# Cluster products, one-hot turns and weight conversions take other tiles of a hand-written attention schedule

## The chip, the cores and the metric

The kernel runs on one core of one Trainium2 chip. The metric is the device time of one execution in microseconds (us); the number that counts is the median of several runs. The core has five engines that run their own instruction queues in order: TensorE (PE in the views, its weight loads PEld), VectorE (DVE), ScalarE (ACT), GpSimd (POOL) and SyncE (SP), which here issues the DMAs.

## The reference

Clustered attention, then two feed-forward stages, all in float32:

```python
q_assign = np.argmax(np.einsum('bhsd,hcd->bhsc', q_n, c_n), axis=-1)   # nearest of 16 centroids
k_assign = np.argmax(np.einsum('bhsd,hcd->bhsc', k_n, c_n), axis=-1)
mask = q_assign[:, :, :, None] == k_assign[:, :, None, :]
scores = np.where(mask, scale * np.matmul(q, k.transpose(0, 1, 3, 2)), -1000000000.0)
attn = softmax(scores)                                  # over keys
x = np.matmul(attn, v)                                  # q, k, v: 2 batches, 8 heads, 768, 64
x = relu(x @ w_in) ** 2 @ w_out                         # 1536 tokens, 512 -> 2048 -> 512
out = sum(p[:, e:e+1] * (relu(x @ w1[e]) @ w2[e]) for e in range(4))
```

## The kernel before

**Stages.** Attention comes first (to about 300 us of the span), then the two feed-forward stages as one long run of matmuls. Every float32 operand is split into a rounded high part and a low part, and products are made of both.

**Attention by tiles.** 16 heads (2 batches by 8) of 6 tiles of 128 queries are 96 tiles, counted by `g`. In tile `g` the program issues: the score products of tile `g+2` (emit_S, L574), the row maximum of tile `g+2` on VectorE (L583), the exponential of tile `g+1` on ScalarE (L594), the turn (transposition) of tile `g`'s probabilities in two halves of three 128x128 transposes (L607), whose results ScalarE (L612, high part `pth`) and VectorE (L613, low part `ptl`) take out of PSUM, and half of the products with `v` of an earlier pair of tiles (L621, L623). The order of these inside a tile is written out by hand in `ORDER`, one list for even and one for odd tiles: `S`, `M`, `E`, `T0`, `T1`, `H`/`L` (results of the turns), `P` (products with `v`), `O` (their results), `R` (loads and DMAs from the table `early`), `C` (one step of the assignment chain from the list `dq`), `K` (one step of a weight conversion). `X1` and `X2` are two places for work of the next heads; `Y1` and `Y2` take their results out of PSUM. All the work at X1 and X2 goes through one PSUM tile, `m`, of a pool with one buffer.

**The preparation of a pair of heads.** Two heads are prepared together, and their work is spread over the 12 tiles before. The tables `AT` (relative to the pair's first tile) and `START` (for the first such pair) say in which tile. I count these 12 tiles as positions 0 to 11, so position 0 is 12 tiles ahead, position 10 two tiles ahead. The parts are:

- turns of k and q (trans_slot, L354), two each at positions 10 and 11 of the cycle before: ScalarE copies each result into `kqf` (L361, three buffers), and GpSimd makes the high and low parts from it (round_pool at L52, then L363) as `nkh`, `nkl`, `nqh`, `nql`;
- cluster products in two halves (pair_scores, L404): keys and queries against the centroids, four matmuls each; ScalarE copies the result to `ys` (L410);
- turns of `ys` in two halves (pair_turn, L420), summed on VectorE into `A` (L425). The second one puts the assignment chain on `dq`: maximum (L456) on VectorE, three GpSimd operations (L446 to L448), two empty steps, second maximum (L457) on VectorE, four GpSimd operations (L451 to L454) that write the one-hot rows `oh`;
- the one-hot turn (pair_hot, L480): `oh` is transposed, ScalarE copies it to `ohm` (L485), and four DMAs (hot_rows, L497) lay its rows under the stacked operands `q2` and `k2` of the pair's first head. The second matmul pair of emit_S reads these;
- stacking DMAs (stack, L375 and L377) that copy parts of `nkh`, `nkl`, `nqh`, `nql` into operands.

The normaliser of the pair that has just ended (norm_slots) uses the same places: its four small VectorE steps (L663 to L666) are put at the head of `dq` at position 2, its turn (L672) comes at position 5, its two broadcasts (L689) at positions 8 and 9. The end of an odd tile issues a DMA of results (L649, `xm`) at position 7.

**The weight conversions.** The first feed-forward weights arrive as 64-bit words, which five VectorE operations (L160, L163, L166, L171, L176, on 128x512 elements), a ScalarE copy and a GpSimd subtraction turn into float32 parts (split64). 24 such steps (four blocks of six) lie in the list `cq` and are done one at a time at `K`, from tile 8 on (`AT["conv"]`). When `cq` is empty, `K` issues pieces of the next weights (`lq`) in tiles with `g % 6 == 4`.

Of the kernel before, what the change touches and what calls it, by code (L numbers as in the profile page):

```python
# [22 lines left out]

ORDER = [
    "S T0 X1 M E T1 R Y1 X2 H0 P0 C H1 L0 L1 C K Y2".split(),
    "S X1 E M T0 T1 Y1 H0 C P1 X2 R L0 H1 C L1 O Y2 C".split()]
WARM = [12, 10, 5, 11, 3, 9]
START = {'t': [0, 1, 1, 2], 'a': [3, 4, 4, 5, 7], 'stack1': 4, 'stack': 5, 'head': [0, 2]}
AT = {"gap": 2, "stack1": -11, "stack": -9, "ohd": -7, "splitv": -3, "load": -8,
      "t": [-14, -14, -13, -13], "a": [-12, -11, -11, -10, -5], "conv": 8}  # L30


@with_exitstack
def moe_attention_kernel(
# [19 lines left out]
    B, H, S, D = q.shape  # L54
    C = centroids.shape[1]
    NT, DM = out.shape
    E = moe2_w1.shape[0]
# [66 lines left out]
    def w_loads(ci):  # L124
        return [(ci, part, half) for part in range(2) for half in range(2)]
# [73 lines left out]
    with tc.manual_schedule():  # L199
# [87 lines left out]
        dq = []  # L287
# [91 lines left out]
        def assign_slot(i):  # L379
            def f():  # L380
                m = ps_m.tile([128, 2 * NTT, 2 * C], F32, tag="m", name="m")
                for j, nm in enumerate(("k1", "q0")):
                    for t in range(NTT):
                        nc.tensor.matmul(
                            m[:, j * NTT + t], stk[i, nm][:, t * 128:(t + 1) * 128],
                            cc[:, i % H], start=True, stop=True)

                def evac():
                    A = as_p.tile([128, 4 * NTT, C], F32, tag="A", name="A")[:, 0:2 * NTT]
                    nc.vector.reduce_sum(  # L390
                        out=A, in_=m.rearrange("p t (s c) -> p t c s", s=2), axis=AX.X)
                    dq.extend(onehot_ops(i, A))
                return evac
            return f
# [130 lines left out]
        def onehot_slot(i):  # L525

            def f():
                while dq:
                    dq.pop(0)()
                om = as_p.tile([128, HALF], F32R, tag="ohm", name="ohm")[0:4 * C]  # L530
                m = ps_m.tile([4 * C, HALF], F32R, tag="m", name="m")
                for a in range(QT):
                    nc.tensor.transpose(
                        m[:, a * 128:(a + 1) * 128],
                        ohs[i][:, 2 * a:2 * a + 2].rearrange("p t s c -> p (t s c)"), identr)

                def evac():
                    nc.scalar.copy(om, m.bitcast(F32))
                    for s, nm in enumerate(("q2", "k2")):
                        for e in range(2):  # L540
                            r = (2 * e + s) * C
                            nc.sync.dma_start(
                                out=stk[i, nm][D:D + C].bitcast(F32).rearrange(
                                    "c (a e n) -> c a e n", a=QT, e=2)[:, :, e],
                                in_=om[r:r + C].bitcast(F32).rearrange("c (a n) -> c a n", a=QT))
                return evac
            return f
# [490 lines left out]
        early, slots = {}, {}  # L1038

        def at(d, g, f):  # L1040
            d.setdefault(max(g, 0), []).append(f)

        for i in range(1, NH):
            u0 = i * NTT
            if i > 1:
                for n, x in enumerate(("stack1", "stack")):
                    at(early, START[x] if i == 2 else u0 + AT[x], lambda i=i, n=n: stack(i, n))
                if i % 2:
                    at(early, u0 + AT["ohd"], lambda i=i: hot_rows(i))
            else:  # L1050
                for n in range(2):
                    at(slots, START["head"][n], onehot_slot(i) if n else assign_slot(i))
            at(early, u0 + AT["splitv"], lambda i=i: split_v(i))
            if i + 1 < NH:
                at(early, u0 + AT["splitv"] + 1, lambda i=i: load_v(i + 1))
        for j in range(1, NH // 2):
            u0 = 2 * j * NTT
            for n, f in enumerate(pair_slots(j)):
                at(slots, START["t"][n] if j == 1 else u0 + AT["t"][n], f)
            for n, f in enumerate([pair_scores(j, 0), pair_scores(j, 1), pair_turn(j, 0),  # L1060
                                   pair_turn(j, 1), pair_hot(j)]):
                at(slots, START["a"][n] if j == 1 else u0 + AT["a"][n], f)
            if j + 1 < NH // 2:
                at(early, u0 + AT["load"], lambda j=j: load_pair(j + 1))
        at(early, 4, lambda: load_w(*w_loads(0)[1]))
        cq, lq = [], []
        for j in range(NF):
# [5 lines left out]
        for g in range(NU):  # L1073
            par = g % 2
            todo = slots.pop(g, [])
            if nq:
                f = nq.pop(0)
                if f is not None:
                    todo.append(f)
            pr, w = divmod(g - 2, 2)  # L1080
            has_pv = 0 <= pr < NU // 2
            end = {}

            def slot(n):
                if todo:
                    end[n] = todo.pop(0)()

            def T(half):
                if g < NU:
                    end["H%d" % half], end["L%d" % half] = emit_T(g, half)  # L1090

            def PV(half):
                if has_pv and w == half:
                    emit_PV(pr, half)

            def PO():
                if has_pv and w == 1:
                    emit_PO(pr)
                    ii, jj = divmod(pr, NTT // 2)
                    if ii % 2 == 1 and jj == NTT // 2 - 1 and pr + 1 < NU // 2:  # L1100
                        nq.extend(norm_slots(ii // 2))

            def other():
                for f in early.pop(g, []):
                    f()

            def convert():
                if g >= AT["conv"] and cq:
                    cq.pop(0)()
                elif not cq and g % NTT == 4:  # L1110
                    for _ in range(2):
                        lq and lq.pop(0)()

            def finish(n):
                f = end.pop(n, None)
                if f:
                    f()

            do = {
                "E": lambda: emit_exp(g + 1), "S": lambda: emit_S(g + 2),  # L1120
                "M": lambda: emit_max(g + 2), "P0": lambda: PV(0), "P1": lambda: PV(1),
                "O": PO, "R": other, "T0": lambda: T(0), "T1": lambda: T(1),
                "X1": lambda: slot("Y1"), "X2": lambda: slot("Y2"),
                "C": lambda: dq and dq.pop(0)(),
                "K": convert,
            }
            for a in ORDER[par]:
                do[a]() if a in do else finish(a)
            while todo:
                whole(todo.pop(0))  # L1130
            if g == NU - 2:
                prep.close()
                mctx = ExitStack()
                for nm in ("w01", "g", "tp"):
                    mp[nm] = mctx.enter_context(
                        tc.tile_pool(name=nm, bufs=1, reuse_waits="tile"))
                w_pool[0, 1] = mp["w01"]
                ga = mp["g"].tile([128, 12 * TB], F32R, name="ga")
                mp["g1"] = ga.rearrange("p (k x t) -> p k x t", k=6, x=2)
                mp["g2"] = ga.rearrange("p (k t) -> p k t", t=HALF)  # L1140
                fa = mp["tp"].tile([128, 6 * HALF + 1024], F32, name="fa")
                mp["r"] = fa[:, 0:2 * TB].rearrange("p (k t) -> p k t", k=2)
                mp["c"] = fa[:, 0:6 * HALF].rearrange("p (k t) -> p k t", k=6)
                sa = fa[:, 6 * HALF:6 * HALF + 1024]
                mp["s"] = sa.rearrange("p (s k f) -> p s k f", s=4, k=2)
                cv_p.append(lambda shp: sa[:, 0:512] if len(shp) == 2 else
                            sa[:, 0:512].rearrange("p (k f) -> p k f", k=shp[1]))
# [55 lines left out]
        def r_ops(b, ops):  # L1203
# [8 lines left out]
        head = {  # L1212
            -1: [("t", RT3), ("t", RT1), ("h", RT1), ("t", RT2), ("l", RT1)],
            0: [("h", RT2), ("h", RT3), ("t", RT4), ("l", RT2)],
            1: [("l", RT3), ("h", RT4), ("h", RB22)],
            2: [("l", RT4), ("l", RB22)]}
# [89 lines left out]
```

## Time and profile before

| | |
|---|---|
| median of 3 runs | 1063.62 us (1061.05 to 1064.61) |
| the profiled execution | 1067.48 us, its span 1065.7 us |
| TensorE busy in the span | 1035.0 us, 97% |
| VectorE, ScalarE, GpSimd busy | 64%, 51%, 52% |
| granted TensorE clock, mean | 0.991 of full |

Busy time of TensorE counts matmuls whose ends are modelled, so 97% doesn't mean that it runs at its peak: a matmul that waits for its predecessor's results shows as a gap, one at a lower clock shows as busy. The span is split at about 300 us: ahead of that all four engines work on attention, after it TensorE has no gap.

### The profile page before, as it was taken

To read this page: it belongs to the slowest core of one execution; us is meant where nothing else is said; L and a number is where in the kernel's file an instruction comes from. 1 tells how busy PE (TensorE), PEld (TensorE's weight loads), DVE (VectorE), ACT (ScalarE), POOL (GpSimd) and SP (SyncE) were. 2 spreads that over 40 slices of the span, in tenths; PEclk is the share of its full clock that TensorE was granted. 3 is DMA by queue.
4 is the path that set the end of the run, shared out by engine and by line. 5 is a ranking of instruction groups with operands and counts; after the bars stand their busy time and mean duration, and the time that the engine had idled before them with its cause. 6 is when DMAs were issued, how large, how long until landed. Compare 5 with 4: busy or idle time off the path is not lost.

```text
span 1065.7 us, 14971 instructions
## 1 busy us (share of the span) xinstructions
PE 1035.0 (97%) x5558; PEld 913.1 (86%) x5558; DVE 684.6 (64%) x1074; ACT 539.7 (51%) x1080; POOL 558.5 (52%) x543
## 2 busy tenths in 40 slices
PE   8899898899999999999999999999999999999998
PEld 7788787888978888888888888899988888889987
DVE  7787787687967676472145555567767555555654
ACT  6678787788855554444344343333354334333331
POOL 3256755665322222224447666667767666666650
PEclk9899999999999999999999999999999999999999
DMA  4664645475212322120102112212213221221201
GB/s 116 146 144 107 139 105 131 112 188 122 48 40 79 113 86 79 40 84 36 40 1 80 65 55 79 79 40 80 79 48 132 79 68 51 79 80 40 79 1 60
DMA packets 72409, 86.07 MB, mean 81 GB/s; under 512 B 26896, under 2 KB 49744, under 8 KB 72336
## 3 DMA queue, kind: packets, MB, share of 16 engines
q1 hardware_dynamic: 72336, 85.11, 28.0%
q8 instruction: 44, 0.72, 0.3%
q14 instruction: 29, 0.24, 0.1%
HBM read 59.83 MB, written 3.15 MB: 59 GB/s over the span
## 4 chain that ended last, share of the span: by engine, by line
PE 83%; DVE 9%; POOL 4%; DMA 2%; issue 1%; ACT 1%; SPq 0%; POOLq 0%; DVEq 0%; ACTq 0%
PE bank L897 25%; PE bank L857 21%; PE bank L750 12%; PE bank L732 4%; PE bank L733 4%; PE bank L731 4%; PE s L574 3%; PE t L607 3%; DVE ptl L613 3%; DVE nb L583 2%; PE po L621 2%; PE po L623 2%; DMA k<-nkh 1%; PE m L404 1%; PE m L689 1%
## 5 line engine op out<-in xcount | busy, mean ns | idle before, releaser
L897 PE MATMUL bank<-w1h,ga 128*128 128x512 f32 x768 | 269.9, 393 | 0.0
L907 DVE SCALAR_TENSOR_TENSOR x<-bank,pe_p,x 128x512 f32<-128x512 f32 x180 | 134.8, 750 | 167.5 <-PE bank L897 167.5
L857 PE MATMUL bank<-xa,w0h 128*128 128x384 f32 x896 | 228.3, 335 | 0.1
L857 PEld LDWEIGHTS bank<-xa,w0h 128*128 128x128 f32 x896 | 164.5, 188 | 17.9 <-ACT fa L868 0.5
L897 PEld LDWEIGHTS bank<-w1h,ga 128*128 128x128 f32 x768 | 144.1, 188 | 24.5
L740 POOL TENSOR_TENSOR ga<-fa,ga 128x512 fp32r<-128x512 f32 x48 | 62.5, 1302 | 177.6 <-ACT ga L739 135.1
L897 PE MATMUL bank<-w1l,ga 128*128 128x512 f32 x384 | 151.6, 395 | 0.0
L857 PE MATMUL bank<-xa,w0l 128*128 128x384 f32 x448 | 149.7, 334 | 0.0
L868 ACT COPY fa<-bank 128x384 f32<-128x384 f32 x96 | 45.6, 475 | 171.6 <-PE bank L857 171.6
L613 DVE TENSOR_TENSOR ptl<-t,pth 128x384 fp32r<-128x384 f32 x192 | 98.8, 549 | 43.8 <-ACT pth L612 43.4
L750 PE MATMUL bank<-ga,w1h 128*128 128x512 f32 x384 | 126.5, 389 | 0.0
L877 ACT ACTIVATE ga<-fa 128x384 fp32r<-128x384 f32 x96 | 50.5, 526 | 135.5 <-DVE fa L871 135.5
L826 POOL TENSOR_TENSOR w0l<-raw,w0h 128x512 fp32r<-128x512 f32 x64 | 75.0, 1194 | 81.2 <-ACT w0h L825 81.2
L844 POOL TENSOR_TENSOR w1l<-raw,w1h 128x1024 fp32r<-128x1024 f32 x32 | 77.3, 2414 | 71.3 <-ACT w1h L843 71.3
L583 DVE TENSOR_REDUCE nb<-s 128x1 f32<-128x768 f32 x96 | 91.2, 950 | 14.9 <-PE s L574 14.2
L607 PE MATMUL t<-identf,p 128*128 128x128 f32 x576 | 89.5, 280 | 6.4 <-DVE ptl L613 5.8
L612 ACT CAST pth<-t 128x384 fp32r<-128x384 f32 x192 | 85.0, 486 | 12.0 <-PE t L607 10.5
L594 ACT ACTIVATE p<-s,nb 128x768 f32<-128x768 f32 x96 | 87.3, 910 | 6.2 <-DVE nb L583 6.0
L880 DVE SCALAR_TENSOR_TENSOR ga<-fa,ga 128x384 fp32r<-128x384 f32 x96 | 90.1, 938 | 0.6 <-ACT ga L877 0.6
L574 PE MATMUL s<-k,q 80*128 80x384 f32 (+1 forms) x384 | 87.7, 351 | 0.2 <-DVE q L327 0.2
L737 ACT ACTIVATE fa<-bank 128x512 f32<-128x512 f32 x44 | 26.4, 599 | 118.0 <-PE bank L733 116.6
L750 PEld LDWEIGHTS bank<-ga,w1h 128*128 128x128 f32 x384 | 72.1, 188 | 14.8
(204 smaller groups left out, 2081.4 us busy)
## 6 DMA issues: line engine op xcount, KB each, us to landing
raw<-in_moe_w_dram SPq DMA_DIRECT2D x64, 512.0 KB, 4.0
raw<-in_moe_w_in_dram SPq DMA_DIRECT2D x8, 1024.0 KB, 5.3
raw<-in_moe_w_out_dram SPq DMA_DIRECT2D x6, 1024.0 KB, 5.0
k<-nkh SPq DMA_DIRECT2D x28, 192.0 KB, 3.3
q<-nqh SPq DMA_DIRECT2D x28, 192.0 KB, 3.6
nv<-in_v_dram SPq DMA_DIRECT2D x16, 192.0 KB, 3.8
out_dram<-x SPq DMA_DIRECT2D x12, 256.0 KB, 2.2
k<-nkl SPq DMA_DIRECT2D x14, 192.0 KB, 3.0
```

The lines of the kernel that those rows point to most:

```text
L574: nc.tensor.matmul(s[:, j, 0:HALF], stk[i, nq][:, t * 128:(t + 1) * 128], stk[i, nk][:, j * HALF:(j + 1) * HALF], start=first, stop=not first)
L583: nc.vector.tensor_reduce(out=nb, in_=s_ps[u][:, :, 0:HALF], axis=AX.XY, op=ALU.max, negate=True)
L594: nc.scalar.activation(p, s_ps.pop(u)[:, :, 0:HALF], AF.Exp, bias=nb_t.pop(u), accum_out=sums_t[hp][:, i % 2, t:t + 1])
L607: nc.tensor.transpose(tp[:, j], p_sb[u][:, half, j * 128:(j + 1) * 128], identf)
L612: return (lambda: nc.scalar.copy(dh, tp), lambda: nc.vector.tensor_tensor(dl, tp, dh.bitcast(F32), op=ALU.subtract))
L613: lambda: nc.vector.tensor_tensor(dl, tp, dh.bitcast(F32), op=ALU.subtract))
L750: nc.tensor.matmul(o, a, b, start=(ft == 0 and z == 0), stop=(ft == NF - 1 and z == 2))
L844: nc.gpsimd.tensor_tensor(lo, w, hi.bitcast(F32), op=ALU.subtract)
L857: nc.tensor.matmul(ps, w[:, o:o + 128], r_op(r, x)[:, kt], start=(first and kt == 0 and z == 0), stop=(kt == 1 and z == 2), skip_group_che ...
L880: nc.vector.scalar_tensor_tensor(out=g_t(n, f, t, 1), in0=h_src(n, f, t), scalar=0.0, in1=g_t(n, f, t, 0).bitcast(F32), op0=ALU.max, op1=A ...
L897: nc.tensor.matmul(o, a, w[:, f], start=(f == 0 and z == 0), stop=(f == 1 and z == 2))
L907: nc.vector.scalar_tensor_tensor(out=acc, in0=o, scalar=pc, in1=acc, op0=ALU.mult, op1=ALU.add)
```

## The change

Four things change. In `AT` and `START` the two cluster products move from positions 0 and 1 to position 2 (both), the turns from positions 1 and 2 to positions 3 and 4, the one-hot turn from position 7 to position 8. For the first such pair the second product and second turn come one tile earlier, and the one-hot turn of head 1 (onehot_slot) takes the second place of its tile. `K` stands in odd tiles too. And `K` does a conversion step only while `dq` is empty.

```diff
-    "S X1 E M T0 T1 Y1 H0 C P1 X2 R L0 H1 C L1 O Y2 C".split()]
+    "S X1 E M T0 T1 Y1 H0 C P1 X2 R L0 H1 C L1 O K Y2 C".split()]
-START = {'t': [0, 1, 1, 2], 'a': [3, 4, 4, 5, 7], 'stack1': 4, 'stack': 5, 'head': [0, 2]}
+START = {'t': [0, 1, 1, 2], 'a': [3, 3, 4, 4, 7], 'stack1': 4, 'stack': 5, 'head': [0, 2]}
-      "t": [-14, -14, -13, -13], "a": [-12, -11, -11, -10, -5], "conv": 8}
+      "t": [-14, -14, -13, -13], "a": [-10, -10, -9, -8, -4], "conv": 8}
...
-                for n in range(2):
-                    at(slots, START["head"][n], onehot_slot(i) if n else assign_slot(i))
+                at(slots, START["head"][0], assign_slot(i))
...
+        at(slots, START["head"][1], onehot_slot(1))
...
                 if g >= AT["conv"] and cq:
-                    cq.pop(0)()
+                    if not dq:
+                        cq.pop(0)()
```

On TensorE, position 0 of the second such pair (tile 12) stood like this before; the four L404 rows are the first half of the cluster products, and the L621 and L623 rows that follow are the products with `v`:

```order
L574 MATMUL s<-k_600,q_663 128x384 x2
L574 MATMUL s<-k_666,q_668 128x384 x2
L607 MATMUL t<-identf,p 128x128 x3
L404 MATMUL m<-nkh,cp 128x384
L404 MATMUL m<-nkl,cp 128x384
L404 MATMUL m<-nqh,cp 128x384
L404 MATMUL m<-nql,cp 128x384
L607 MATMUL t<-identf,p 128x128 x3
```

Of the change, TensorE at position 2 (tile 14):

```order
L574 MATMUL s<-k_605,q_663 128x384 x2
L574 MATMUL s<-k_666,q_668 128x384 x2
L607 MATMUL t<-identf,p 128x128 x3
L404 MATMUL m<-nkh,cp 128x384
L404 MATMUL m<-nkl,cp 128x384
L404 MATMUL m<-nqh,cp 128x384
L404 MATMUL m<-nql,cp 128x384
L607 MATMUL t<-identf,p 128x128 x3
L404 MATMUL m<-nkh,cp 128x384
L404 MATMUL m<-nkl,cp 128x384
L404 MATMUL m<-nqh,cp 128x384
L404 MATMUL m<-nql,cp 128x384
```

The same eight rows now stand two tiles later, and the second half follows in the same tile after only three transposes.

On VectorE, positions 4 to 7 of that pair before; L456 and L457 are the chain's two maxima, L176 is a conversion step:

```order
L456 TENSOR_REDUCE mx<-A 128x24
L583 TENSOR_REDUCE nb<-s 128x1
L613 TENSOR_TENSOR ptl<-t,pth 128x3x128 x2
L176 SCALAR_TENSOR_TENSOR cva<-raw,cva 128x512
L583 TENSOR_REDUCE nb<-s 128x1
L613 TENSOR_TENSOR ptl<-t,pth 128x3x128
L457 TENSOR_REDUCE mx_1557<-A 128x24
L613 TENSOR_TENSOR ptl<-t,pth 128x3x128
L583 TENSOR_REDUCE nb<-s 128x1
```

Of the change, VectorE from the same maximum on (positions 4 to 7); L163 and L166 are conversion steps:

```order
L456 TENSOR_REDUCE mx<-A 128x24
L583 TENSOR_REDUCE nb<-s 128x1
L613 TENSOR_TENSOR ptl<-t,pth 128x3x128 x2
L583 TENSOR_REDUCE nb<-s 128x1
L457 TENSOR_REDUCE mx_1127<-A 128x24
L613 TENSOR_TENSOR ptl<-t,pth 128x3x128 x2
L163 TENSOR_SCALAR cva<-cva 128x512
L583 TENSOR_REDUCE nb<-s 128x1
L613 TENSOR_TENSOR ptl<-t,pth 128x3x128 x2
L166 TENSOR_SCALAR cva<-cva 128x512
```

The conversion between the two maxima is gone, and one conversion stands in each tile from the second maximum's on.

On SyncE's queue, the DMAs around the one-hot rows (`ohm`) of that pair before:

```order
L497 DMA q_1089<-ohm 16x3x128 x2
L497 DMA k_1087<-ohm 16x3x128 x2
L375 DMA k_1247<-nkh 64x768
L377 DMA k_1247<-nkl 64x768
L649 DMA xm<-xs 64x768
L375 DMA q_1335<-nqh 64x768
```

And of the change:

```order
L375 DMA k_1240<-nkh 64x768
L377 DMA k_1240<-nkl 64x768
L649 DMA xm<-xs 64x768
L497 DMA q_1085<-ohm 16x3x128 x2
L497 DMA k_1083<-ohm 16x3x128 x2
L375 DMA q_1338<-nqh 64x768
```

The four one-hot DMAs have moved behind three others, two of the next head's stack and the one of results.

## Rows read from the trace of the kernel before

**Rows 1.** Windows of ten tiles, positions 0 to 9, of six pairs; columns as printed.

```profile
core 0: us, PE busy (x) PEld busy (x) DVE busy (x) ACT busy (x) POOL busy (x), PEclk, DMA share, GB/s
59.66:87.68 28.02, 26.00 (x188) 23.29 (x186) 23.62 (x43) 22.83 (x53) 16.51 (x22) 1.00 0.50 113
93.60:122.02 28.42, 25.98 (x187) 23.30 (x186) 23.61 (x43) 22.84 (x53) 16.92 (x23) 1.00 0.49 109
127.94:158.44 30.50, 27.72 (x188) 24.88 (x186) 23.71 (x43) 22.86 (x53) 17.42 (x23) 0.94 0.44 98
164.36:195.38 31.02, 27.77 (x188) 24.78 (x186) 23.25 (x42) 22.84 (x53) 17.90 (x24) 0.94 0.47 109
201.30:231.51 30.21, 27.27 (x187) 24.89 (x186) 20.95 (x39) 22.01 (x52) 16.46 (x25) 0.94 0.56 136
237.43:264.64 27.21, 25.50 (x187) 23.38 (x186) 20.86 (x39) 21.92 (x52) 15.06 (x24) 1.00 0.49 121
```

**Rows 2.** Windows of single tiles: positions 0 and 1, position 1, a plain tile.

```profile
201.30:207.59 6.29, 3.87 (x23) 2.99 (x22) 1.64 (x4) 2.73 (x7) 5.96 (x8) 0.97 0.51 134
207.59:211.97 4.38, 4.38 (x24) 4.28 (x24) 2.42 (x5) 2.49 (x7) 0.01 (x1) 0.66 0.00 0
242.03:245.06 3.03, 3.03 (x26) 2.99 (x24) 2.40 (x5) 2.58 (x8) 0.20 (x1) 1.00 0.00 0
268.79:270.86 2.07, 2.07 (x18) 2.04 (x17) 1.87 (x4) 1.89 (x6) 0.12 (x1) 1.00 0.59 160
```

**Rows 3.** Waits over the span: who waited for whom, us, times, longest.

```profile
PE m L404 <- POOL nql L363: 3.8, 6, 0.6
PE m L404 <- POOL nqh L52: 3.8, 5, 0.9
...
ACT kqf L361 <- POOL nkl L363: 2.5, 3, 1.3
...
PE m L480 <- DVE oh L466: 1.9, 1, 1.9
```

**Rows 4.** Windows of positions 4 and 6 with conversions, position 6 without.

```profile
71.44:74.07 2.63, 2.52 (x19) 1.97 (x17) 2.63 (x7) 2.25 (x6) 0.62 (x1) 1.00 0.98 208
76.31:79.95 3.64, 2.51 (x19) 1.96 (x17) 3.64 (x7) 2.37 (x6) 3.50 (x5) 1.00 0.75 167
220.81:223.05 2.24, 2.24 (x18) 2.02 (x17) 2.24 (x5) 2.04 (x6) 2.24 (x3) 1.00 1.04 231
```

**Rows 5.** Windows of positions 7, 8, 10 and 11, and of a position 2.

```profile
79.95:82.26 2.31, 2.31 (x21) 2.28 (x20) 1.75 (x4) 2.31 (x6) 1.69 (x3) 1.00 0.03 7
82.26:84.97 2.71, 2.71 (x21) 2.43 (x20) 1.92 (x4) 2.45 (x7) 0.43 (x1) 1.00 0.13 27
87.68:90.94 3.26, 2.95 (x25) 2.68 (x23) 2.40 (x5) 2.93 (x9) 2.92 (x6) 1.00 0.97 202
90.94:93.60 2.66, 2.66 (x25) 2.62 (x23) 2.64 (x4) 2.21 (x7) 2.44 (x3) 1.00 0.81 198
245.06:247.55 2.49, 2.49 (x23) 2.45 (x22) 2.47 (x7) 2.22 (x6) 1.52 (x2) 1.00 0.41 86
```

**Rows 6.** VectorE timeline, GpSimd timeline, and line L176: ns min/median/max, first and last.

```profile
75.08 1.45 DVE L176 SCALAR_TENSOR_TENSOR cva<-raw,cva 128x512 int32<-128x512 int32 x1
...
74.98 1.01 POOL L448 TENSOR_TENSOR A<-A,wgt 128x384 f32<-128x384 f32 x1
...
L176 DVE SCALAR_TENSOR_TENSOR cva<-raw,cva x18: 691/692/1825, 75.1 to 471.6; 128x512 int32<-128x512 int32 x18
```

**Rows 7.** One-hot rows at position 7: ScalarE and SyncE timeline, then all their DMAs' landing.

```profile
81.22 0.48 ACT L485 CAST ohm<-m 128x384 fp32r<-128x384 f32 x1
...
81.72 1.34 SPq L497 DMA_DIRECT2D q<-ohm  x2
83.10 1.23 SPq L497 DMA_DIRECT2D k<-ohm  x2
...
DMA to landing us min/median/max: 1.9/2.0/4.7
```

## The prediction

> **What bounds the kernel now.** The page comes first: TensorE is the busy engine throughout, and after attention it has no gap, so only attention can give anything, and what it gives reaches the end in full, because the feed-forward stages are bound by TensorE and start when attention ends. Then the timeline by tiles, each from its first score product to the next one's. A plain tile takes 2.07 us [rows 2], TensorE busy throughout; VectorE (1.87) and ScalarE (1.89) have some 0.2 to spare. So a tile's price is TensorE's as long as VectorE's extra work is small, and VectorE becomes the price where it isn't. Then windows of positions 0 to 9 [rows 1]: the six full pairs take 28.02, 28.42, 30.50, 31.02, 30.21 and 27.21 us, 175.4 in all, with 25.50 to 27.77 of TensorE busy in each, some of it at half clock.
>
> Three things make them long. **First**, position 0, 6.29 us in the worst case [rows 2]: the cluster products stand there while GpSimd still makes the low and high parts of q. The waits [rows 3] show TensorE stopped by `nqh` and `nql` 11 times for 7.6 us (gaps of the matmuls alone; the loads ahead wait longer). **Second**, the clock after it: position 1 takes 4.38 us at a granted clock of 0.66, where the same work takes 3.03 at 1.00 [rows 2], so the two levels (1.2 and 2.4 GHz) cost 1.35 there. Ahead of the fall TensorE had only 3.87 of 6.29 us busy. Three of the six pairs show 0.94 over ten tiles, the others 1.00 [rows 1]. **Third**, positions 4 and 6 in the four pairs with conversions: 2.63 and 3.64 us with VectorE busy throughout, where position 6 without one takes 2.24 [rows 4].
>
> **The sum of a pair after the change.** Ten tiles at 2.07 are 20.7. The work at X1 and X2 on top, by what a tile exceeds a plain one: product and turn together 0.96 (3.03 - 2.07) [rows 2]; a turn 0.42 (2.49) [rows 5]; so the other product about 0.54; the one-hot turn 0.24 (2.31); two broadcasts of the normaliser at 0.64 (2.71) [rows 5]; its small turn, one transpose where the one-hot turn has three, 0.1. That is 3.54. Two new waits come in, because both products stand in one even tile (position 2), and the one-hot turn now shares an even tile (position 8) with a broadcast. The second of such a couple waits until ScalarE has emptied the single `m` buffer, with only three transposes between. The row for this is the even tile with two turns of k, 3.26 us, against 2.66 for two turns in an odd tile [rows 5], where more stands between: 0.60 each, 1.2 a pair. Below, the wait could be nothing if ScalarE is early; above, twice that (the products' result queues behind an exponential). I take 0.6, the same copy in the same place. Sum: 20.7 + 3.54 + 1.2 = 25.4 a pair, 152.6 for six. **Saved: 175.4 - 152.6 = 22.8.** This contains the products' waits, the half clock behind them and the stalls of positions 4 and 6; positions 10 and 11 keep their price. Why should the products not wait two tiles on? Positions 0 and 1 will be plain, 4.14 together, where position 0 alone took 4.2 to 6.3 with GpSimd finishing within it; with the scores of position 2 ahead that leaves GpSimd at the latest half a microsecond short for the second half, which itself comes after the first half and the buffer wait. I put 0.5 for the six.
>
> **What is given back.** (a) *Conversions.* The chain is on `dq` at positions 3, 4 and 5 when `K` comes, so nine of twelve tiles take a step, before six. The 24 steps end at tile 37 instead of 54. VectorE is busy 20.9 us in a pair without conversions [rows 1], so it has 4.6 spare in 25.4, and about 1.5 more at positions 10 and 11. Nine steps, seven or eight of them on VectorE, want 4.5 to 7.5. That is about all there is, and plain tiles (0, 1, 6, 7) can't hide a step of 0.4 to 1.4 in 0.2. VectorE can run late by some two microseconds before TensorE stops, an estimate from position 6 without conversion: VectorE is busy for all of its 2.24 us, behind the whole chain, and TensorE too [rows 4]. Going from tile to tile by these prices, it is caught up at positions 2, 8 and 10 and over at 4, 6, 0 and 1, and the stalls come to 2.5 with steps at their short duration and 6 at their long one. Bounds: nothing, and 12 (16 of the 20 VectorE steps lengthening their tiles by 0.75). I take 5.
>
> The long duration: L176 took 1.45 us at 75.08 while GpSimd ran L448, against a median of 0.69 over all 18 [rows 6]. More steps will stand at positions where GpSimd is at work. The Trainium skill ("SBUF — State Buffer", section "SBUF: two separate sides") gives the rule: a VectorE instruction with two SBUF inputs and a GpSimd instruction exclude each other for the whole instruction. The trace agrees for this row (0.76 longer than the median, of the 0.91 for which L448 ran on). By the rule alone every step at a busy position would pay it, which is the first rival below; with the short durations the sum would be 2.5 better.
>
> (b) *ScalarE held by `kqf`.* The fourth turn of k and q waits for GpSimd to release a buffer, 2.5 us in three waits, the longest 1.3 [rows 3]. Until now TensorE stood at position 0 anyway; now the exponential and the `pth` copies of plain tiles queue behind it on ScalarE, and TensorE waits for these. Between nothing and 2.5; I take 2.5, since the plain tile leaves ScalarE 0.18.
>
> (c) *One-hot rows.* Before, the copy began 1.27 after its tile's start, the DMAs left from 81.72 to 84.33, and the last landed 1.9 to 2.0 after its own start (83.7), at about 85.6, 5.7 after the tile's start at 79.95 [rows 5, 7]. Now the turn stands in position 8 behind three transposes (0.3), so 6.0. The first reader is the second half of the scores at position 10, 0.36 in: 3.55 (2.07 + 0.24 + 0.64 + 0.6) + 2.71 + 0.36 = 6.6. There is 0.6 to spare; the slowest landing (4.7) would make it 2.1 late. Three DMAs now stand ahead in SyncE's queue; the results' one waits for a ScalarE copy from the end of position 7, which is done before the one-hot copy on the same engine. I take 0.5 in all, with bounds 0 and 6 times 2.1.
>
> (d) *The first pair.* Its one-hot turn waits 1.9 for the VectorE chain [rows 3]. Second product and turn come one tile sooner, so VectorE gets the sums about 0.6 sooner; the turn of head 1 stands behind a turn of q instead of ahead of it and waits in its shade. I take a gain of 1 (bounds -0.5 and 3).
>
> The conversions' earlier end brings the next weights' pieces forward (first at tile 40, not 58); they go at the same positions, and nothing waits for them in attention, so 0.
>
> **Sum:** 22.8 - 0.5 - 5 - 2.5 - 0.5 + 1 = 15.3 from 1067.5, which is 1052.2. The median of the runs shown is 3.9 below this execution. Its half-clock stretches may be more than a usual run has; those inside the six pairs are in the 22.8 already, two at the start stay in my sum and a usual run may lack one (about 1.3, as above). So **1051**.
>
> **Rivals.** *VectorE becomes the bound while conversions last* (for it: rows 6 and the spare above; against: 22 tiles of it only). The upper bound of (a), 7 more: 1058. Chance 0.17. *Nothing is given back* (for it: VectorE's tolerance, waits of (b) caught up at position 2): (a) 1, (b) and (c) nothing, (d) 2 because the clock holds at the start: 22.8 - 0.5 - 1 + 2 = 23.3 and 1044. Chance 0.15. *The change doesn't do what it says*: GpSimd isn't done at position 2 either, because it gets a conversion's subtraction in between, so the products wait some 2 a pair, as at position 0 in the slowest tile's three gaps: 12 back, 1063. Against: 4 us of delay. Chance 0.05. *Slower*: one-hot rows too late. If the results' DMA ahead holds SyncE's queue for a tile (2.7) the rows land 2.1 late, and with the slow landing 4.8; the scores stop, and the clock falls behind it (1.35): 3.5 to 6.2 a pair, at 4.5 27 for six, 1079. It decides from 3 a pair on. Against: 0.6 spare, and the copy it waits for is older than the one-hot's. Chance 0.05.
>
> **How the numbers follow.** The forecast holds 0.58, and by itself reaches from 1046 to 1056 (terms (a) to (d) at half their bounds). Differences under 0.3% (3.2 us) can't be told from no change here. Faster by more: forecast, first and second rival, 0.9; same 0.05; slower 0.05. A range of 1042 to 1059 takes in the forecast and the first two rivals and leaves out less than 2 in 10.
>
> **What would show it.** Right: no wait of L404 for `nqh` or `nql`; clock 1.00 from 60 to 300 us; pairs of 25 to 27 us; a gap of about 0.3 before the second product at position 2 and before the broadcast at position 8; L176 and L163 longer than alone at positions 7 to 0. Wrong: waits of L574 for a DMA from `ohm` at position 10; TensorE stopped by `ptl` for more than 8 us in all; attention ending later than about 288 us instead of some 300.

## The result and the profile after

The changed kernel takes 1052.41 us (median of 4 runs, 1051.82 to 1053.16), the kernel before 1064.11 in the runs made beside it (1061.05 to 1064.77). The ratio is 0.9896, with a 95% interval of 0.9875 to 0.9917: faster, 1.0%. The forecast was 1051.0, within 1042 to 1059. The profiled execution took 1052.45, against 1052.2 by the sum. In the medians the gain is 11.7, in the spans below 15.3, because the profiled execution of before (1067.48) stood 3.4 above its median and this one is at its own. The page of the changed kernel:

```profile
span 1050.4 us, 14956 instructions
PE 1029.3 (98%) x5558; PEld 908.4 (86%) x5558; DVE 684.1 (65%) x1074; ACT 539.3 (51%) x1080; POOL 560.4 (53%) x543
```

The span is 15.3 us shorter (1065.7 before). The windows of positions 0 to 9 of the six pairs (length; TensorE, its weight loads, VectorE, ScalarE and GpSimd busy; granted clock; DMA) answer to [rows 1]:

```profile
59.77:86.34 26.57, 25.87 (x188) 23.25 (x186) 24.73 (x45) 22.73 (x53) 16.82 (x21) 1.00 0.56 126
92.25:120.80 28.55, 26.61 (x188) 23.11 (x186) 25.48 (x45) 22.87 (x53) 19.25 (x24) 1.00 0.52 117
126.72:153.87 27.15, 26.04 (x187) 23.15 (x186) 23.12 (x41) 22.78 (x53) 17.20 (x23) 1.00 0.61 141
159.98:185.84 25.86, 25.40 (x188) 23.35 (x186) 20.88 (x39) 22.07 (x52) 14.85 (x22) 1.00 0.64 154
191.76:217.58 25.82, 25.36 (x188) 23.35 (x186) 20.86 (x39) 22.02 (x52) 14.94 (x23) 1.00 0.58 136
223.50:249.34 25.84, 25.38 (x188) 23.38 (x186) 20.87 (x39) 22.05 (x52) 14.94 (x23) 1.00 0.43 99
```

The sum is 159.8 instead of 175.4, so the pairs save 15.6 and the rest of the program loses 0.3. The clock is 1.00 in all six. The last three pairs have no conversions and agree to 0.04: 25.84 is the price of a clean pair. The first three exceed it by 0.73, 2.71 and 1.31, 4.75 together: that much goes with the conversions, and a run below takes most of them out.

Single tiles of the changed kernel: positions 0, 1, 2 and 8 of clean pairs, then positions 1 and 2 of the second pair and position 2 of the third:

```profile
159.98:162.13 2.15, 2.15 (x19) 2.12 (x18) 1.53 (x4) 2.11 (x6) 2.01 (x4) 1.00 0.47 118
162.13:164.29 2.16, 2.16 (x18) 2.00 (x17) 2.16 (x4) 2.13 (x5) 2.05 (x3) 1.00 0.63 137
164.29:168.28 3.99, 3.75 (x26) 3.44 (x25) 2.62 (x5) 3.02 (x8) 1.95 (x3) 1.00 0.40 99
179.85:183.13 3.28, 3.06 (x24) 2.71 (x23) 2.52 (x5) 3.08 (x8) 0.13 (x2) 1.00 0.79 208
94.59:98.06 3.47, 2.53 (x16) 2.04 (x17) 3.47 (x6) 2.63 (x6) 3.30 (x5) 1.00 0.50 112
98.06:102.55 4.49, 3.97 (x27) 3.38 (x26) 4.00 (x8) 3.12 (x8) 2.93 (x5) 1.00 0.36 89
131.10:135.84 4.74, 3.96 (x26) 3.36 (x25) 3.70 (x7) 3.54 (x9) 4.14 (x5) 1.00 0.35 86
```

Positions 0 and 1, which held the products' waits and the half clock behind them in [rows 2], are now nearly plain. Position 2 holds both products and a TensorE gap of 0.24. Where conversions last, positions 1 and 2 are 0.50 to 1.31 longer than the same tiles of a clean pair; these three rows hold 2.56 of the 4.75.

TensorE's waits over the span (who waited for whom: us, times, longest), and one of ScalarE, answer to [rows 3]:

```profile
PE t L607 <- DVE ptl L613: 3.2, 7, 0.9
...
PE m L533 <- DVE oh L520: 2.0, 1, 2.0
PE m L480 <- DVE oh L466: 1.9, 1, 1.9
...
PE m L689 <- ACT ohm L485: 1.5, 6, 0.5
PE m L404 <- ACT ys L410: 1.4, 6, 0.2
...
PE m L420 <- DVE A L425: 0.5, 1, 0.5
...
ACT kqf L361 <- POOL nkl L363: 0.9, 2, 0.6
```

L404 no longer waits for `nqh` or `nql` (7.6 before). In their place stand the two small waits for the single `m` buffer, L404 for `ys` and L689 for `ohm`. The first pair's L480 still waits 1.9, and L533, the one-hot turn of head 1, waits longer than before (1.24 there).

### The profile page after: what moved, and what is told of

Read it like the earlier page. It is cut to its first block, busy times and chain, and to the rows that moved or that the text cites. A ratio compares the mean times of both kernels' runs of the same rounds, so it can differ in the third digit from the quotient of the medians.

```text
span 1050.4 us, 14956 instructions
## 1 busy us (share of the span) xinstructions
PE 1029.3 (98%) x5558; PEld 908.4 (86%) x5558; DVE 684.1 (65%) x1074; ACT 539.3 (51%) x1080; POOL 560.4 (53%) x543
## 4 chain that ended last, share of the span: by engine, by line
PE 86%; DVE 6%; DMA 2%; ACT 2%; SPq 1%; POOL 1%; issue 1%; ACTq 0%; POOLq 0%; DVEq 0%
PE bank L897 25%; PE bank L857 22%; PE bank L750 12%; PE bank L733 4%; PE s L574 4%; PE bank L731 4%; PE bank L732 4%; PE t L607 3%; PE po L621 2%; PE po L623 2%; DVE ptl L613 2%; DVE nb L583 1%; PE m L404 1%; DMA k<-nkh 1%; SPq L236 1%
## 5 line engine op out<-in xcount | busy, mean ns | idle before, releaser
L750 PEld LDWEIGHTS bank<-ga,w1h 128*128 128x128 f32 x384 | 72.1, 188 | 14.7
```

What stands on the lines that cost most here:

```text
L750: nc.tensor.matmul(o, a, b, start=(ft == 0 and z == 0), stop=(ft == NF - 1 and z == 2))
```

## The experiments

The theory: most of the gain comes from moving the cluster products behind GpSimd's rounding of q; the conversion rule takes 3 to 6 us of stalls away when it stands alone, and what it costs in the change comes from VectorE running late. The rivals: the conversion rule makes the gain and the products' wait only moves, or crowded steps cost as much as they save.

**Turns alone, conversions alone.** The first kernel has only the new `AT` row, the second only the two edits of `K`.

```diff
-      "t": [-14, -14, -13, -13], "a": [-12, -11, -11, -10, -5], "conv": 8}
+      "t": [-14, -14, -13, -13], "a": [-10, -10, -9, -8, -4], "conv": 8}
```

> Only the positions of products, turns and one-hot turn of the later pairs are changed; conversions and the first pair stay as before. Theory (the products waited for GpSimd, and the clock fell behind that wait): pairs without conversions take 25.8 us as in the change, product waits for nqh and nql are gone, the clock stays at 1.00 from 60 us on, and the four pairs keep most of the 7.8 us of VectorE stalls at positions 4 and 6: 12 to 13 us faster than before. Rival (the conversions' move made the gain, the products' wait only moves): 0 to 5 us faster, with waits of L404 for nqh and nql still there.

> Only K in odd tiles and the rule that a conversion waits for an empty chain are taken over; products, turns and one-hot turn stay where they were before. Theory: the steps fall into tiles 8 to 37, the stalls at positions 4 and 6 (7.8 us) go, some come back in plain tiles, while positions 0 and 1, where TensorE waits for GpSimd anyway, hide theirs: 3 to 6 us faster than before, product waits and half-clock stretches as before. Rival (crowded steps cost as much as they save): within 2 us of before.

Turns alone: 1048.9 us, ratio 0.986 (0.9845 to 0.9875), six pairs 160.1, each at a clock of 1.00, with no wait of L404 for `nqh` or `nql`. That is 15.2 faster where 12 to 13 were expected; the start, below, has the rest. Conversions alone: 1062.8, ratio 0.9987 (0.9974 to 1.0), six pairs 171.8. TensorE's waits of the second:

```profile
PE m L404 <- POOL nqh L52: 4.8, 6, 0.9
PE m L404 <- POOL nql L363: 3.8, 6, 0.6
PE m L480 <- POOL oh L454: 3.5, 6, 0.8
```

So the conversion rule alone shortens the pairs by 3.6 against the profiled execution of before, part of it because that one had three pairs at a clock of 0.94 [rows 1] and this one has two; the products' waits stay, the wait of L480 for GpSimd's `oh` grows (1.0 in two before, 3.5 in six), and the medians differ by 1.3, which can't be told from no change. The 3 to 6 us expected of the rule are missed, and the rival on crowded steps holds. In the change the pairs are 0.3 shorter than with turns alone (159.8 against 160.1), and the kernel with turns alone is 3.5 faster. The pairs don't explain that difference. The windows of the first twelve tiles do: 40.59 in the changed kernel and 37.08 with turns alone.

```profile
19.18:59.77 40.59, 35.10 (x238) 32.17 (x237) 30.84 (x59) 27.51 (x64) 11.07 (x15) 0.92 0.53 126
```

```profile
19.59:56.67 37.08, 32.35 (x238) 29.02 (x237) 30.17 (x58) 27.14 (x64) 9.66 (x13) 1.00 0.55 130
```

Nearly the same work (the start's edits and the conversion steps of the last tiles differ), at a granted clock of 0.92 above and 1.00 below. TensorE's gaps are 0.8 longer above, its busy time 2.7.

**The start as before.** In the changed kernel, `START` and the place of head 1's one-hot turn are those of before.

```diff
-START = {'t': [0, 1, 1, 2], 'a': [3, 3, 4, 4, 7], 'stack1': 4, 'stack': 5, 'head': [0, 2]}
+START = {'t': [0, 1, 1, 2], 'a': [3, 4, 4, 5, 7], 'stack1': 4, 'stack': 5, 'head': [0, 2]}
...
-                at(slots, START["head"][0], assign_slot(i))
+                for n in range(2):
+                    at(slots, START["head"][n], onehot_slot(i) if n else assign_slot(i))
...
-        at(slots, START["head"][1], onehot_slot(1))
```

> The change with the first pair's part undone (second product, second turn, and the one-hot turn of head 1 at their old places). Theory from the trace of the change, where tiles 2 to 9 together took 0.4 us longer than before: 0 to 1 us faster than the change. Rival (the prediction's term for the first pair, a gain of 1 us): 1 us slower than the change.

1051.14 us, ratio 0.9879; pairs 159.8, as in the changed kernel; first twelve tiles 38.62 at a clock of 0.96. So the start edits lose about 1.3 us by the medians (the two intervals overlap) and 2.0 in the windows, where I had forecast a gain. Of the 2.0, 0.8 are gaps of TensorE and 1.2 its busy time at the lower clock. The VectorE rows of the changed kernel at the start (start, duration, instruction) show where the gaps come from, with the row of TensorE that waits for them:

```profile
27.07 0.94 DVE L583 TENSOR_REDUCE nb<-s 128x1 f32<-128x768 f32 x1
27.94 0.72 DVE L519 TENSOR_SCALAR oh<-off 128x96 fp32r<-128x96 f32 x1
28.58 0.60 DVE L520 TENSOR_TENSOR oh<-A,mx 128x96 fp32r<-128x96 f32 x1
29.33 0.34 PE L533 MATMUL m<-identr,oh 128*64 128x128 f32 x3 [1.96 <-DVE oh L520]
```

The same of the kernel before:

```profile
27.52 0.40 DVE L519 TENSOR_SCALAR oh<-off 128x96 fp32r<-128x96 f32 x1
27.83 0.25 DVE L520 TENSOR_TENSOR oh<-A,mx 128x96 fp32r<-128x96 f32 x1
...
28.00 0.94 DVE L583 TENSOR_REDUCE nb<-s 128x1 f32<-128x768 f32 x1
28.22 0.35 PE L533 MATMUL m<-identr,oh 128*64 128x128 f32 x3 [1.24 <-DVE oh L520]
```

The later place in the tile lets a row maximum (0.94) go ahead of the one-hot rows on VectorE, and these two run longer (0.72 and 0.60 against 0.40 and 0.25). Why they do isn't shown: GpSimd rounds q beside them in both kernels.

**Most of the conversions left out.** In the changed kernel the second to fifth VectorE operation of each of the four blocks is not done (16 of 20 are missing; the weights of these blocks aren't computed).

```diff
-            cq += [f for fs in split64(0, 0, j, cv_p[0]) for f in fs]
+            cq += [f if n in (0, 5) else (lambda: None) for n, f in enumerate(
+                f for fs in split64(0, 0, j, cv_p[0]) for f in fs)]
```

> The change with 16 of the 20 VectorE steps of the weight conversion left out (the second to fifth operation of each block; their places stay empty steps), so the weights of the first block are not computed. Theory (conversions cost 4.7 us in the change): all six pairs take 25.8 to 26.2 us and the kernel is 4 to 5 us faster than the change. Rival (what the pairs with conversions have on top comes from kqf, or from the one-hot rows): within 1 us of the change.

1048.81 us, ratio 0.9858; pairs 156.7, 3.1 less, with the same start (40.60 at 0.92). The medians differ by 3.6, less than the 4 to 5 expected. The first pair becomes clean (25.86); the second keeps 1.26 of its 2.71. Of this, 0.83 is at position 1, where VectorE waits, and 0.42 at position 8, where ScalarE's copy of the conversion (L182), which this kernel still does, stands ahead of the exponential and the one-hot copy. The timeline of the changed kernel at position 1 of that pair:

```profile
92.11 1.01 POOL L363 TENSOR_TENSOR nkl<-kqf,nkh 128x384 fp32r<-128x384 f32 x1
...
93.09 1.28 POOL L184 TENSOR_TENSOR w0l<-cva,w0h 128x512 fp32r<-128x512 f32 x1
...
94.40 0.73 DVE L160 TENSOR_SCALAR cva<-raw 128x512 int32<-128x512 int32 x1 [1.60 <-POOL w0l L184]
...
95.05 0.94 DVE L583 TENSOR_REDUCE nb<-s 128x1 f32<-128x768 f32 x1
95.91 1.00 DVE L613 TENSOR_TENSOR ptl<-t,pth 128x384 fp32r<-128x384 f32 x2
...
96.51 1.01 PE L607 MATMUL t<-identf,p 128*128 128x128 f32 x6 [0.94 <-DVE ptl L613]
```

The first step of a block (L160) writes `cva`, of a pool with one buffer, which the GpSimd subtraction of the block before (L184) still reads. That subtraction stands in GpSimd's queue behind the rounding of k. VectorE stops for 1.60 us, the row maximum and `ptl` queue behind it, and TensorE stops for 0.94. With steps in neighbouring tiles this wait appears (1.6 in the changed kernel, 0.9 in this one, 2.0 with conversions alone); in the kernel before and with turns alone, with one step in two tiles, it is 0. A second buffer for `cva` was not tried.

**The products split, and one tile later only.** Two other rows of the table on the kernel before, without the conversion rule: products at positions 2 and 3, so that they don't share a tile; and everything one tile earlier than in the change (both products at position 1, so the first moves by one tile and the second stays; turns at 2 and 3). The two new rows stand below one another.

```diff
-      "t": [-14, -14, -13, -13], "a": [-12, -11, -11, -10, -5], "conv": 8}
+      "t": [-14, -14, -13, -13], "a": [-10, -9, -9, -8, -4], "conv": 8}
...
+      "t": [-14, -14, -13, -13], "a": [-11, -11, -10, -9, -5], "conv": 8}
```

> Turns only, and of the two products the second one tile later, in odd position 3 ahead of the first turn, so that no even tile holds both; conversions and first pair as before. Theory (the second of two works at X1 and X2 of an even tile waits about half a microsecond for ScalarE to empty m): positions 2 to 4 take about 0.6 us less a pair, the wait of L404 for ys is gone, 3 to 4 us faster than turns only. Rival (the chain, now half a tile later, makes the one-hot turn at position 8 wait, or VectorE's lateness eats it): within 1 us of turns only.

> Turns only, but everything one tile earlier than in the change: both products at odd position 1, turns at 2 and 3, one-hot turn at its old position 7. Theory (GpSimd ends nqh and nql of the second half about 10 to 11 us after the start of position 10, and what matters is that the products come after that): the first half still waits some 0.5 us a pair, the second hardly, the clock stays at 1.00, no wait of the second product for ys in an odd tile; the one-hot turn waits for GpSimd's oh again by about 0.5: within 3 us of turns only. Rival (the delay needed is the full two tiles): product waits of over 1 us a pair and half-clock stretches: 5 to 12 us slower than turns only.

Split: **1046.16 us**, ratio 0.9835 (0.982 to 0.985), six pairs 155.1, 5.0 less than with turns alone. By the medians it is 2.7 faster than turns alone, below the 3 to 4 expected, in part because its start (38.62) took 1.5 longer. It is the fastest of all. Positions 2 and 3 of one of its pairs:

```profile
158.73:161.66 2.93, 2.93 (x23) 2.64 (x22) 2.15 (x5) 2.12 (x6) 1.78 (x3) 1.00 0.41 100
161.66:164.68 3.02, 3.02 (x26) 2.98 (x24) 2.98 (x7) 2.57 (x8) 0.00 (x0) 1.00 0.56 130
```

TensorE is busy throughout in both, and the wait of L404 for `ys` is gone from its list. The wait for `ptl` falls to 1.3 in three (turns alone 3.3 in eight), so the shared tile also made VectorE late.

One tile later: 1051.09, ratio 0.9884, pairs 160.4. TensorE's waits:

```profile
PE t L607 <- DVE ptl L613: 6.7, 15, 0.7
...
PE m L404 <- POOL nql L363: 0.5, 2, 0.3
```

The 7.6 of before all stood at the first product, at position 0; one tile of delay removes nearly all of it, and the pairs are as long as with turns alone (160.4 and 160.1). The later places shorten the stalls behind `ptl` (6.7 to 3.3) and bring the waits for `ys` and `ohm` at the shared tiles (1.4 and 1.3). In all they take 2.2 off TensorE's gaps in the pairs and add 1.8 to its busy time; where these 1.8 come from isn't shown. Most of the 2.2 us by which the medians differ is the start again: this kernel's first twelve tiles take 38.63 at a clock of 0.96.

**Conversions in spare tiles.** If a tile with a turn or a broadcast has slack on VectorE, steps belong there: turns alone, and the split products, each with steps only at positions 2 and 8 to 11 (`K` in both lists).

```diff
-                    cq.pop(0)()
+                    if g % 12 in (2, 8, 9, 10, 11):
+                        cq.pop(0)()
```

> Turns only, and conversion steps in even and odd tiles, but only at positions 2, 8, 9, 10 and 11 of the twelve, the tiles that last longer than VectorE's own work; first pair as before. Theory (a step costs TensorE only where the tile leaves VectorE no time, by position and not by the chain's list): of the 5 us of VectorE stalls in the pairs 3 to 5 go, waits of L607 for ptl nearly vanish: 3 to 5 us faster than turns only. Rival (steps are lengthened at these positions because GpSimd works there, or VectorE's total is what counts): within 1 us.

> Both of the two before: second product at position 3, conversions at positions 2, 8, 9, 10 and 11. If both effects are real and independent, 6 to 9 us faster than turns only; if position 2, shorter by one product, no longer has the time for its step, 1 to 2 us less than the two together.

That theory fell: 1051.85 and 1047.61 us, 3.0 and 1.5 slower than their bases; pairs 161.7 (base 160.1) and 157.8 (155.1). The steps of the first kernel by line (busy, mean; VectorE idle before them and for what):

```profile
L160 DVE TENSOR_SCALAR cva<-raw 128x512 int32<-128x512 int32 x3 | 2.4, 793 | 3.9 <-POOL w0l L184 3.9
```

It is the wait of L160 for GpSimd's subtraction again, 3.9 in two here and 3.7 in the second kernel: with four steps in a row the next block's first step comes while the subtraction still stands in GpSimd's queue, behind the rounding of v in one case and of k in the other.

**The change with split products; and steps where GpSimd is idle.** The first kernel is the changed one with -9 for the second -10. The second is the split one with the same six steps a pair, in tiles 1, 2, 3, 4, 7 and 8 of twelve.

> This is the change with one number altered: the second cluster product goes to position 3 instead of position 2, so that the two products no longer share a tile. If the price of the shared tile is separate from that of the conversions, the six pairs lose what the clean pair shows for it (25.84 of the change against 25.33 to 25.62 of the turns with split products, about 0.4 a pair) plus the ys waits (1.4 us), so about 157 instead of 159.8 and some 1049.5 us. If the shared tile is the reason why VectorE's lateness reaches TensorE at positions 1 and 2 while conversions last, the conversion stalls shrink too: pairs 155 to 156, 1047 to 1048. If the crowding by conversions sets the pairs alone, nothing changes: 1052.

> The split products (1046.2 us, pairs 155.1) with as many conversion steps a pair, six, but in tiles 1, 2, 3, 4, 7 and 8 of twelve, where GpSimd is idle for most of positions 3, 4 and 8, instead of every second tile. If the length that a step takes on beside GpSimd's instructions is what costs, the steps are shorter and the extra of the conversion pairs (about 3 us over six pairs against the clean pairs of 25.3 to 25.6) falls: pairs 153 to 154, 1044 to 1045. If steps in neighbouring tiles cost because VectorE gets no plain tile to catch up, whatever GpSimd does, the pairs grow to 157 or more and the time to 1048 or more.

The first: 1049.17 us, ratio 0.986 (0.9845 to 0.9874), pairs 157.0. The clean pairs fall to 25.3 and the second pair stays at 28.31 with L160's wait of 1.6: the two prices are separate, as the first theory had it. The second: 1048.13, ratio 0.9851, pairs 159.4, 4.2 above its base. By line its steps (60 to 250 us) take 0.64 on average (12.2 for 19), in the base 0.71 (12.8 for 18), in the changed kernel 0.86 (14.7 for 17); the shortest steps go with long pairs. Positions 4 and 8 of one pair (base 2.62 and 3.28):

```profile
132.99:136.12 3.13, 2.70 (x22) 2.43 (x21) 3.10 (x8) 2.21 (x6) 0.00 (x0) 1.00 0.95 209
143.28:146.99 3.71, 3.06 (x25) 2.71 (x24) 2.55 (x6) 3.51 (x9) 1.58 (x3) 1.00 0.27 58
```

Position 4 is long because VectorE makes the sums of the turns there and has a step right ahead of them and another a tile before (3.10 of 3.13 busy; L420 waits 1.7 for `A`, nothing in the base). Position 8 is long because the ScalarE copy of the conversion falls there and the exponential and the one-hot copy queue behind it (L689 waits 3.1 for `ohm` instead of 1.3). So here neighbouring steps cost, though GpSimd is mostly idle and L160 does not wait; but the ScalarE copy shares in it, so the test doesn't price VectorE's crowding alone.

## Why the prediction was right, step by step

**What bounds it, and the products' waits: right.** The waits for `nqh` and `nql` and the half clock inside the pairs are gone, and the span falls by what the pairs fall. Turns alone give 15.3 of the pairs' 15.6. Of the signs named, the pairs of 25 to 27 us are missed twice (28.55 and 27.15), where conversions last.

**The sum of a pair: 25.4 forecast, 25.84 measured.** Saved by the clean price: 175.4 - 6 x 25.84 = 20.4 instead of 22.8, and 20.4 - 4.75 = 15.6 as the windows have it. The term that was mis-sized is the plain tiles at 2.07: positions 0, 1, 6 and 7 take 2.15, 2.16, 2.24 and 2.34, with TensorE busy throughout (at 1, 6 and 7 VectorE too), 0.6 together above their price; [rows 4] had 2.24 for position 6 already. Position 2 takes 3.99 where the terms make 3.75 (2.07, two products at 0.54, the wait at 0.6). TensorE's gap in it is 0.24, not 0.6: the wait was oversized and the work undersized. Position 8 came out at 3.28 for 3.55, again with a gap of 0.22 in place of 0.6.

**(a) Conversions: 5 forecast, 4.75 measured, part of it by another mechanism.** Leaving out 16 of 20 operations returns 3.1 of it, so VectorE's work and what it delays is most. But of the positions named for the stalls (4, 6, 0 and 1) only 1 is a main one (1.8 over the three pairs); 0 and 4 have 0.2 and 0.5, 6 nothing, and position 2, where VectorE was to have caught up, has 1.5. And the largest single one (1.31 at position 1 of the second pair) comes with a dependence that I had not looked for, L160 on GpSimd's subtraction. That the total came out within 0.3 is in part luck. The forecast price of one operation beside GpSimd was right in kind: L163 takes 0.99 at 96.84, with L363 on GpSimd, and 0.42 on average with turns alone. The Trainium skill ("SBUF — State Buffer", section "SBUF: two separate sides") names two SBUF inputs or a two-port mode as what excludes GpSimd. L163 has one input, so of the two cases only the mode could cover it; no run here shows in which mode it ran. So the rule on two inputs, as the prediction has it, covers L171 and L176 and not every step.

**(b) ScalarE held by `kqf`: 2.5 forecast, nothing measured.** This step failed: the wait was taken over at its old length. ScalarE's wait for `nkl` fell from 2.5 to 0.9, and TensorE has no gap at positions 0 and 1 of a clean pair. The lower bound was the right end.

**(c) One-hot rows: 0.5 forecast, nothing measured.** The last copy and DMAs before position 10 of one pair:

```profile
213.06 0.48 ACT L485 CAST ohm<-m 128x384 fp32r<-128x384 f32 x1
213.57 1.35 SPq L497 DMA_DIRECT2D q<-ohm  x2
...
214.97 1.22 SPq L497 DMA_DIRECT2D k<-ohm  x2
...
217.58 0.69 PE L574 MATMUL s<-k,q 128*128 128x384 f32 x3
```

The last DMA starts at some 215.6 and lands 2.0 later by the median, at 217.6; its reader is 0.36 behind 217.58. It fits by 0.3, and no score product waits for it. The rival on the other side was that near.

**(d) The first pair: a gain of 1 forecast, a loss of 0.45 measured** (40.14 to 40.59, windows of the first twelve tiles). This step failed. That the turn of head 1 would wait "in the shade" of a turn of q was wrong, because VectorE is in order and a row maximum came ahead. Against the kernel before, TensorE's gaps grew by 0.8, and its busy time fell by 0.3. The bound of -0.5 just held against that start, which ran at 0.91 itself; against the start as before in the same kernel (38.62) it did not: 2.0.

The total was nearer than its terms: the clean pair (2.4 too good) and (d) (1.4) stood against (b), (c) and the products' remainder (3.5 too bad). That these cancel is luck. The step from 1052.2 to 1051 took 1.3 off for a fall of the clock at the start that a usual run would lack; it does not lack it, the median equals the profiled execution.

**The rivals.** VectorE as the bound: no, 4.75 and not 12. Nothing given back: not here, though the split products, another kernel, come close to its time (1046.16 against 1044). The change doing nothing, or the rows landing late: no.

## What to carry to other kernels

When a consumer waits for a producer on another engine, the least delay that covers the wait is enough; past that, look at what the moved work now shares a tile and a buffer with. Here one number, -9 for -10, which keeps two users of a single buffer apart, took 2.7 us off turns alone and 3.2 off the change. Before background steps are spread over more slots, follow their own chain through its other engines: a step that waits for a busy engine holds everything behind it on an in-order queue, and the pauses between steps had hidden that here.

## What the runs showed of the hardware that I had not expected

The same start of the program, the first twelve tiles, ran at a mean granted clock of 1.00 (37.1 us) in the profiled executions of three kernels, 0.96 (38.6) in five, and 0.91 or 0.92 (40.1 to 40.6) in four: with no fall of the clock, one and two. Nine of the twelve have the same instructions there up to the first conversion steps (tile 8), and they are spread over all three levels of the result. In the changed kernel the tile ahead of a fall had TensorE busy for 3.31 of 5.35 us, and the next ran at 0.69, a mean of time at 1.2 and at 2.4 GHz:

```profile
25.08:30.43 5.35, 3.31 (x25) 2.70 (x24) 5.03 (x10) 3.63 (x10) 5.10 (x8) 0.97 0.00 2
30.43:35.32 4.89, 4.89 (x25) 4.79 (x25) 1.98 (x3) 2.36 (x6) 1.23 (x2) 0.69 0.29 76
```

With turns alone TensorE is busy for 3.29 of 4.83 us in the tile ahead, with the wait of 1.24 as before (and 1.9 some tiles on), and no fall follows. This early fall is in all three kernels that have the change's start, with its wait of 2.0, and of the nine others in the kernel before alone. Nor is a kernel's start fixed: the four runs of the change with the start as before list a clock of 0.997 to 1.000 over the span. What decides between them stays open. Each fall costs about 1.5 us (37.08, 38.6, 40.1), as much as several of the edits tried here, so kernels within 2 us of each other are better compared by their pair windows than by their times.
